# When the gathers of the tile three on are issued in a mixture-of-experts stage: a quarter into the tile instead of at its start

## The chip, the cores and the metric

The kernel runs on one core of a Trainium2 chip. Its engines are named as in the profile: PE (TensorE; PEld is its weight load), DVE (VectorE), ACT (ScalarE), POOL (GpSimd) and SP (SyncE). The metric is the device time of one execution in microseconds; the time before is the median of three runs.

## The reference

A squared-relu attention without softmax makes a gated x, and a mixture of experts with one expert a token is applied to it. Of the reference, cut:

```
scores = (1/S) * z @ z.T                 # B = 8, S = 2496, d_qk = 64
attn   = maximum(scores, 0) ** 2
x      = (u * (attn @ v)).reshape(B*S, 256)

logits = x @ w_gate                      # 8 experts
e      = argmax(logits); gate = softmax(logits)[e]
for each expert e:                       # w1[e]: 256 x 1024, w2[e]: 1024 x 256
    h  = maximum(x[mask] @ w1[e], 0)
    out[mask] = gate[mask] * (h @ w2[e])
```

## The kernel before

The span has two parts. Up to about 1400 us the attention is worked off. Its rows of x (256 numbers, the gate and the token's place, 272 words a row) are written to the DRAM tensor `xrows`, and the tokens are sorted by expert into lists of places. From there to the end the **expert tiles** run, 47 of them in a list `order`, 0 to 46. The first six ("A") are drawn from all sequences but the last, the others ("F") from what remains. A tile is 4, 3 or 2 blocks of 128 tokens of one expert. More tiles follow behind a branch on the number that the data needs; they don't run in the profiled execution.

A tile `i` goes through these steps, each a function:

- `load_w` (L701): an expert's weights come in two halves, each an indirect DMA of 128 × 2048 numbers that POOL issues.
- `load_x(i)` (L711): for each block an indirect DMA, issued by POOL, gathers 128 rows of `xrows` into a buffer `rows`, of which there are three. These are the **gathers**.
- `turn_x(i)` (L742): for each block a transposing DMA, issued by SP, from `rows` to `th`, of which there are three too.
- `take_gates(i)` (L747): DVE copies the gates out of `rows` into `gt`, and with that `rows` is used up.
- `split_x(i)` (L755 and L758 on ACT, L756 and L759 on DVE): the turned halves are put together and split into a high and a low part for PE.
- `split_piece` (L731 to L734): ACT and DVE split a piece of the weights in the same manner.
- `up` (PE L776 into `ph`; then ACT's relu L780 and DVE's subtraction L781, which make its high and low part), `down` (PE L799 for the high part, L802 for the low one, into `y`).
- `finish(i)` (ACT L812, DVE L813, and then L815): the result is weighted with the gates, and for each block POOL issues an indirect DMA that writes 128 rows to the output. These are the **scatters**.

A tile of 4 or 3 blocks has 8 groups of hidden columns, a tile of 2 blocks has 4. The loop in `tiles` goes over tiles and groups, `g` being the group and `G` their number in the tile. In each group PE does `up` for the group two on and `down` for this one. At `g == 0` the weights of the next expert and the gathers of tile `i + 3` are issued, at `g == G // 2` tile `i + 2` is turned and its gates taken, at `g == 0` tile `i + 1` is split, and the last group finishes the tile.

The order of the program is not the order on an engine. Each engine works off its own queue in order, and a scheduler fills these queues: it may put an instruction that stands later in the program ahead of others, as its own reckoning of when operands are ready has it. `pinned(work)` (L350) takes that freedom from what it is given: each instruction is issued behind the last instruction of every engine among the 400 that were written just before. Indirect DMAs all go through POOL's one queue: gathers, scatters and weight halves hold each other up there by their order.

Of the kernel before, what the change touches and what calls it, by code (L numbers as in the profile page):

```python
# [47 lines left out]
def fused_kernel(ctx: ExitStack, tc: tile.TileContext, zt, ut, v, wg, wcat, out):  # L48
# [40 lines left out]
    def ring_rows():  # L89
        return sb.tile([P, QC // P, ROW], I32, name="rows", tag="rows", bufs=3)  # L90

    def ring_sd():
        return sb.tile([P, QC // P, ROW], I32, name="sd", tag="sd")
# [256 lines left out]
    def pinned(work):  # L350

        last = {}
        for i in nc.cur_bb.bb.instructions[-400:]:
            last[i.engine] = i
        with ExitStack() as behind:
            for i in last.values():
                behind.enter_context(tc.issue_after(i))
            work()
# [338 lines left out]
    def load_w(w, h):  # L697
        which, t, _ = order[first_of[w]]
        wr = slot(free[0])
        free.append(free.pop(0))  # L700
        nc.gpsimd.indirect_dma_start(out=wr, out_offset=None, in_=wcat,  # L701
                                     in_offset=bass.IndirectOffsetOnAxis(ap=lists[which]["widx"][:, h, t:t + 1], axis=0))
        weights[w, h] = wr

    def load_x(i):
        which, t, k = order[i]
        src = xrows[0:NTOK - S, :] if which == "A" else xrows

        xg = ring_sd() if i == 0 else ring_rows()
        for s in range(k):  # L710
            nc.gpsimd.indirect_dma_start(out=xg[:, s, :], out_offset=None, in_=src,  # L711
                                         in_offset=bass.IndirectOffsetOnAxis(ap=lists[which]["idx"][:, s, t:t + 1], axis=0))
        xgs[i] = xg

    def split_piece(q):

        i, j = divmod(q, NPC)
        wr = weights[i, j // 2]
        jj = j % 2
        if q % 6 < 5:  # L720
            w1, w2 = ring4(), ring4()
        else:

            if not kept:
                kept.append(free.pop(0))
            w12 = slot(kept[0]).bitcast(FR)
            w1, w2 = [w12[:, k * F:(k + 1) * F].rearrange("p (a b d) -> p a b d", a=2, b=2) for k in range(2)]

        r1 = wr[:, 0:F].rearrange("p (i f) -> p i f", i=2)[:, :, jj * FP:(jj + 1) * FP]
        r2 = wr[:, F:].rearrange("p (c d) -> p c d", d=D)[:, 2 * jj:2 * jj + 2, :]  # L730
        nc.scalar.copy(w1[:, 0], r1)  # L731
        nc.vector.tensor_tensor(w1[:, 1], r1, w1[:, 0].bitcast(F32), op=ALU.subtract)
        nc.scalar.copy(w2[:, :, 0, :], r2)
        nc.vector.tensor_tensor(w2[:, :, 1, :], r2, w2[:, :, 0, :].bitcast(F32), op=ALU.subtract)  # L734
        pieces[q] = w1, w2

    def turn_x(i):

        k = blocks[i]
        tp = ring_halves()  # L740
        for s in range(k):
            nc.sync.dma_start_transpose(out=tp[:, :, s * P:(s + 1) * P], in_=xgs[i][:, s, 0:D].bitcast(U16))  # L742
        turned[i] = tp

    def take_gates(i):
        gates[i] = sb.tile([P, BS], F32, name="gt", bufs=4)
        nc.vector.tensor_copy(gates[i][:, 0:blocks[i]], xgs.pop(i)[:, 0:blocks[i], D].bitcast(F32))  # L747

    def split_x(i):

        n = blocks[i] * P
        tp = turned.pop(i)
        xf = sb.tile([P, 2, QC], F32, name="x", tag="x")
        halves = xf[:, :, :n].bitcast(U16).rearrange("p i (n h) -> p i n h", h=2)
        nc.scalar.copy(halves[:, :, :, 1], tp[:, 0:2, :n])  # L755
        nc.vector.tensor_copy(halves[:, :, :, 0], tp[:, 2:4, :n])  # L756
        xh, xl = ring_hi(), ring_lo()
        nc.scalar.copy(xh[:, :, :n], xf[:, :, :n])  # L758
        nc.vector.tensor_tensor(xl[:, :, :n], xf[:, :, :n], xh[:, :, :n].bitcast(F32), op=ALU.subtract)  # L759
        xts[i] = xh, xl  # L760

    def up(gi):
        i, g = groups[gi]
        n = blocks[i] * P
        w1 = pieces[piece_of[gi]][0]
        xh, xl = xts[i]
        ph = ps1.tile([P, QC], F32, name="ph", tag="ps1")
        m = fs_of[i]
        for c in range(m):
            f = g * m + c  # L770
            fs = slice(f % 2 * P, (f % 2 + 1) * P)
            o = ph[:, c * n:(c + 1) * n]
            p = 0
            for dd in range(2):
                for part, xx in ((0, xh), (0, xl), (1, xh)):
                    nc.tensor.matmul(o, lhsT=w1[:, part, dd, fs], rhs=xx[:, dd, :n], start=p == 0, stop=p == 5)  # L776
                    p += 1
        hh, hl = ring2(), ring2()
        m *= n
        nc.scalar.activation(hh[:, :m], ph[:, :m], AF.Relu)  # L780
        nc.vector.scalar_tensor_tensor(hl[:, :m], ph[:, :m], 0.0, hh[:, :m].bitcast(F32),  # L781
                                                     op0=ALU.max, op1=ALU.subtract)
        return hh, hl

    def down(gi, hh, hl):
        i, g = groups[gi]
        k = blocks[i]
        n = k * P
        w2 = pieces[piece_of[gi]][1]
        if g == 0:  # L790
            yts[i] = [ps2.tile([P, 2, QC], F32, name=f"y{s}", tag="ps2") for s in range(-(-k // 2))]
        for h in (hh, hl):
            for c in range(fs_of[i]):
                f = g * fs_of[i] + c
                for s in range(k):
                    y = yts[i][s // 2][:, s % 2, :]
                    cs = slice(c * n + s * P, c * n + (s + 1) * P)
                    if h is hh:
                        nc.tensor.matmul(y, lhsT=h[:, cs], rhs=w2[:, f % 2].rearrange("p i d -> p (i d)"),  # L799
                                         start=f == 0, stop=False)  # L800
                    else:
                        nc.tensor.matmul(y[:, 0:D], lhsT=h[:, cs], rhs=w2[:, f % 2, 0, :], start=False,  # L802
                                         stop=f == NF - 1)

    def finish(i):
        which, t, k = order[i]
        gt = gates.pop(i)
        yo = ring_f().rearrange("p a (b d) -> p (a b) d", d=D)
        for s in range(k):
            y = yts[i][s // 2][:, s % 2, :]  # L810
            gate = gt[:, s:s + 1]
            nc.scalar.mul(yo[:, s, :], y[:, D:2 * D], gate)  # L812
            nc.vector.scalar_tensor_tensor(yo[:, s, :], y[:, 0:D], gate, yo[:, s, :], op0=ALU.mult, op1=ALU.add)  # L813
        for s in range(k):
            d = nc.gpsimd.indirect_dma_start(  # L815
                out=out, out_offset=bass.IndirectOffsetOnAxis(ap=lists[which]["idx"][:, s, t:t + 1], axis=0),
                in_=yo[:, s, :], in_offset=None, bounds_check=NTOK - 1, oob_is_err=False)
            for o in outs:
                tc.declare_no_dep(d.ins, o.ins, reason="rows are distinct")
            outs.append(d)  # L820
# [93 lines left out]
    def tiles(lo, hi, n_pieces):  # L914

        mine = [gi for gi, (i, _) in enumerate(groups) if lo <= i < hi]
        for gi in mine:
            i, g = groups[gi]
            G = NF // fs_of[i]
            if bg:  # L920
                pinned(bg.pop(0))
            if g == 0:

                for w, h in ((wof[i] + 1, 0), (wof[i] + 1, 1), (wof[i] + 2, 0)):
                    if own[i] and w <= wof[hi - 1] and (w, h) not in weights and (w < NA or i > NA):
                        load_w(w, h)
                if i + 3 < hi:
                    load_x(i + 3)
            ahead = min(gi + LU, mine[-1])
            while n_pieces < min(piece_of[ahead] + LP + 1, NPC * (wof[hi - 1] + 1)):  # L930
                split_piece(n_pieces)
                n_pieces += 1
            if i + 2 < hi and g == G // 2:
                turn_x(i + 2)
                take_gates(i + 2)
            if i + 1 < hi and g == (0 if i else G // 2):
                pinned(lambda: split_x(i + 1))
            if gi + LU <= mine[-1]:
                hs[gi + LU] = up(gi + LU)
            down(gi, *hs.pop(gi))  # L940
            if g == G - 1:
                finish(i)

    tiles(0, NM, n_pieces)
    needed = nc.values_load(lists["F"]["ns"], min_val=0, max_val=NS)

# [56 lines left out]
```

## Time and profile before

| | |
|---|---|
| runs | 2322.43, 2313.3, 2318.6 us; median 2318.6 |
| profiled execution | 2324.7 us, of which 2322.9 are the span |
| granted TensorE clock, mean | 0.994 |
| PE busy | 2278.9 us, 98% |
| DVE busy | 1632.0 us, 70% |
| ACT busy | 1465.3 us, 63% |
| POOL busy | 625.7 us, 27% |
| gathers of F tiles (L711) | 136, 138.9 us of POOL's time |
| scatters (L815) | 136 of F tiles and 24 of A tiles, 143.7 and 25.3 us |
| weight halves (L701), from 1400 us on | 66, 69.5 us |

A view by windows gives each engine's busy time in a stretch of the span. The timeline has one row for an instruction or for a few of a kind in a row: start, duration, engine, line, operation, what is written and read, and in brackets how long the engine stood idle before it and what ended that. "issue" there is time in which the engine waited for nothing that the profile shows. A matmul's end is modelled, so that neighbouring ones overlap by some tenths.

### The profile page before, as it was taken

The page shows a single profiled execution, that of the slowest core. Times are in us where ns is not written, and L with a number is a line of the kernel's source. Part 1 is how long each engine was busy: PE and PEld are TensorE (multiplying, and loading weights), DVE is VectorE, ACT ScalarE, POOL GpSimd, SP SyncE. Part 2 cuts the span into 40 slices and gives each one's busy share as a digit, 9 for nine tenths or more (in the row PEclk, how much of TensorE's full clock was granted, in tenths as well). Part 3 has the DMA queues.
Part 4 walks back from the last instruction along what each step waited for, and adds up shares of the span by engine and source line. Part 5 has one row for each costly group of instructions (what it writes and reads, how often), then busy time and mean ns, then how long its engine had stood idle before and what let it go on. Part 6 is the DMA issues. An engine that isn't in the chain of part 4 may idle for free.

```text
span 2322.9 us, 33688 instructions
## 1 busy us (share of the span) xinstructions
PE 2278.9 (98%) x12320; PEld 1925.6 (83%) x12320; DVE 1632.0 (70%) x2909; ACT 1465.3 (63%) x1985; POOL 625.7 (27%) x626
## 2 busy tenths in 40 slices
PE   9999999999999999999999989899999999999998
PEld 7888888888888888888888877688888888888887
DVE  8868868878778778877878766455566656657554
ACT  8768668677677777767776654355465555546454
POOL 1011111112102102102111244543445435345322
PEclk9999999999999999999999999899999999999999
DMA  6556656657567367467375484654566646457620
GB/s 163 104 92 135 97 86 135 93 95 134 85 105 132 80 116 121 79 118 125 79 114 95 121 176 89 189 123 131 154 152 173 176 128 207 134 146 194 151 89 29
DMA packets 454366, 287.31 MB, mean 124 GB/s; under 512 B 389100, under 2 KB 411130, under 8 KB 444976
## 3 DMA queue, kind: packets, MB, share of 16 engines
q1 hardware_dynamic: 422800, 165.98, 40.0%
q0 software_dynamic: 31392, 119.10, 17.6%
q8 instruction: 98, 1.61, 0.4%
q14 instruction: 76, 0.62, 0.1%
HBM read 149.79 MB, written 43.43 MB: 83 GB/s over the span
## 4 chain that ended last, share of the span: by engine, by line
PE 85%; issue 4%; DMA 3%; ACT 3%; DVE 2%; POOL 1%; another core or an unknown queue 1%; SPq 0%; POOLq 0%; ACTq 0%
PE ph L776 16%; PE acc L343 13%; PE acc L346 13%; PE acc L345 13%; PE y L799 11%; PE y L802 6%; PE ps_s L306 4%; PE ps_s L307 4%; DMA vr<-in_v_dram 2%; PE ps_s L278 2%; PE pt L398 1%; POOL out_dram L815 1%; PE ps_s L312 1%; DMA rows<-xrows,laidx 1%
## 5 line engine op out<-in xcount | busy, mean ns | idle before, releaser
L346 PE MATMUL acc<-thi,t 128*128 128x512 f32 (+1 forms) x1600 | 614.3, 386 | 0.0
L343 PE MATMUL acc<-thi,t 128*128 128x512 f32 (+1 forms) x1600 | 608.0, 392 | 1.1 <-issue 0.7
L345 PE MATMUL acc<-tlo,t 128*128 128x512 f32 (+1 forms) x1520 | 586.0, 386 | 0.1
L781 DVE SCALAR_TENSOR_TENSOR t<-ph,t 128x512 fp32r<-128x512 f32 (+1 forms) x328 | 220.3, 675 | 238.1 <-ACT t L780 192.5
L776 PE MATMUL ph<-thi,t 128*128 128x512 f32 (+2 forms) x1248 | 379.3, 361 | 3.8 <-issue 2.1
L780 ACT ACTIVATE t<-ph 128x512 fp32r<-128x512 f32 (+1 forms) x328 | 191.9, 591 | 289.1 <-PE ph L776 210.4
L346 PEld LDWEIGHTS acc<-thi,t 128*128 128x128 f32 x1600 | 300.2, 188 | 55.3 <-DVE t L140 0.6
L343 PEld LDWEIGHTS acc<-thi,t 128*128 128x128 f32 x1600 | 299.5, 188 | 54.4 <-DVE x L366 1.2
L345 PEld LDWEIGHTS acc<-tlo,t 128*128 128x128 f32 x1520 | 285.6, 188 | 50.8 <-DVE tlo L319 0.7
L476 POOL DMA_INDIRECT lst<-toks,posi x160 | 197.0, 1231 | 468.2 <-DVE posi L468 425.8
L799 PE MATMUL y<-t,t 128*128 128x512 f32 x1062 | 306.3, 397 | 13.5 <-DVE t L734 6.4
L776 PEld LDWEIGHTS ph<-thi,t 128*128 128x128 f32 x1248 | 226.1, 189 | 32.9 <-issue 2.9
L799 PEld LDWEIGHTS y<-t,t 128*128 128x128 f32 x1062 | 191.5, 191 | 48.7 <-ACT t L780 7.8
L776 PE MATMUL ph<-tlo,t 128*128 128x512 f32 (+2 forms) x624 | 225.6, 362 | 0.7 <-issue 0.7
L815 POOL DMA_INDIRECT out_dram<-tf,lfidx x136 | 143.7, 1057 | 273.4 <-DVE tf L813 245.5
L802 PEld LDWEIGHTS y<-t,t 128*128 128x128 f32 x1062 | 175.8, 190 | 35.2 <-DVE t L781 5.7
L802 PE MATMUL y<-t,t 128*128 128x256 f32 x1062 | 185.0, 283 | 3.6 <-DVE t L781 3.6
L315 ACT ACTIVATE tf<-ps_s 128x1024 f32<-128x1024 f32 (+1 forms) x145 | 133.8, 923 | 85.3 <-PE ps_s L307 43.3
L307 PE MATMUL ps_s<-t,t 128*128 128x512 f32 (+1 forms) x480 | 178.9, 376 | 0.0
L380 POOL MEMSET rows<- 128x64 int32 x40 | 6.8, 172 | 581.7 <-DMA xrows<-rows 359.6
L317 DVE CAST thi<-tf 128x1024 fp32r<-128x1024 f32 (+1 forms) x145 | 90.9, 627 | 102.3 <-ACT tf L316 94.5
L711 POOL DMA_INDIRECT rows<-xrows,lfidx x136 | 138.9, 1021 | 50.2 <-issue 38.3
(252 smaller groups left out, 4050.2 us busy)
## 6 DMA issues: line engine op xcount, KB each, us to landing
vr<-in_v_dram SPq DMA_DIRECT2D x80, 256.0 KB
xrows<-rows SPq DMA_DIRECT2D x32, 544.0 KB
u<-in_ut_dram SPq DMA_DIRECT2D x32, 512.0 KB
zr<-in_zt_dram SPq DMA_DIRECT2D x38, 256.0 KB
u<-in_ut_dram SPq DMA_DIRECT2D x8, 448.0 KB
xrows<-rows SPq DMA_DIRECT2D x8, 408.0 KB
rows<-th SPq DMA_TRANSPOSE x160
lst<-toks,posi POOLq DMA_INDIRECT x160
```

The costliest lines, as they stand in the source:

```text
L307: nc.tensor.matmul(ps[:, i, m:n], lhsT=hl_k, rhs=lh_q[:, m:n], start=False, stop=True)
L343: nc.tensor.matmul(acc[d][:, :n], lhsT=vh, rhs=hi[:, i, :n], start=first and i == 0, stop=False)
L345: nc.tensor.matmul(acc[d][:, :n], lhsT=vh, rhs=lo[:, i, :n], start=False, stop=False)
L346: nc.tensor.matmul(acc[d][:, :n], lhsT=vl, rhs=hi[:, i, :n], start=False, stop=last and i == 1)
L476: i = nc.gpsimd.indirect_dma_start(out=lst1, out_offset=bass.IndirectOffsetOnAxis(ap=posi[:m, j:j + 1], axis=0), in_=toks[:m, col + j:col ...
L711: nc.gpsimd.indirect_dma_start(out=xg[:, s, :], out_offset=None, in_=src, in_offset=bass.IndirectOffsetOnAxis(ap=lists[which]["idx"][:, s, ...
L776: nc.tensor.matmul(o, lhsT=w1[:, part, dd, fs], rhs=xx[:, dd, :n], start=p == 0, stop=p == 5)
L780: nc.scalar.activation(hh[:, :m], ph[:, :m], AF.Relu)
L781: nc.vector.scalar_tensor_tensor(hl[:, :m], ph[:, :m], 0.0, hh[:, :m].bitcast(F32), op0=ALU.max, op1=ALU.subtract)
L799: nc.tensor.matmul(y, lhsT=h[:, cs], rhs=w2[:, f % 2].rearrange("p i d -> p (i d)"), start=f == 0, stop=False)
L802: nc.tensor.matmul(y[:, 0:D], lhsT=h[:, cs], rhs=w2[:, f % 2, 0, :], start=False, stop=f == NF - 1)
L815: d = nc.gpsimd.indirect_dma_start(out=out, out_offset=bass.IndirectOffsetOnAxis(ap=lists[which]["idx"][:, s, t:t + 1], axis=0), in_=yo[:, ...
```

## The change

The call `load_x(i + 3)` is taken out of the part for `g == 0`. It now stands behind it under `g == G // 4`, which is the third group of a tile with 8 groups and the second of a tile with 4, and it is wrapped in `pinned`.

```diff
                 for w, h in ((wof[i] + 1, 0), (wof[i] + 1, 1), (wof[i] + 2, 0)):
                     if own[i] and w <= wof[hi - 1] and (w, h) not in weights and (w < NA or i > NA):
                         load_w(w, h)
-                if i + 3 < hi:
-                    load_x(i + 3)
+            if g == G // 4 and i + 3 < hi:
+                pinned(lambda: load_x(i + 3))
             ahead = min(gi + LU, mine[-1])
```

On PE and ACT the order of instructions stays as it was, but for buffer numbers. On POOL it moves. The first place is where the gathers of tiles 6 to 11 stand. In the rows, `rows<-xrows,lfidx` is a gather, `out_dram<-tf` a scatter and `s_` a weight half; the number behind x counts instructions in a row. POOL before, from the gathers of tiles 6 to 9 (6 of them, a weight half, 8 more) over the scatters of tile 3, the gathers of tile 10, the scatters of tile 4 and the gathers of tile 11:

```order
L711 DMA rows<-xrows,lfidx 128x272 x6
L701 DMA s_15482<-in_wcat_dram,lfwidx 128x2048
L711 DMA rows<-xrows,lfidx 128x272 x8
L815 DMA out_dram<-tf,laidx 19968x256 x2
L701 DMA s_15620<-in_wcat_dram,lfwidx 128x2048
L815 DMA out_dram<-tf,laidx 19968x256 x2
L711 DMA rows<-xrows,lfidx 128x272 x2
L815 DMA out_dram<-tf,laidx 19968x256 x4
L711 DMA rows<-xrows,lfidx 128x272 x4
L701 DMA s_15622<-in_wcat_dram,lfwidx 128x2048
```

POOL now, at the same place, from the gathers of tiles 6 and 7 over the scatters of tiles 3 and 4 to the gathers of tiles 8, 9 and 10:

```order
L711 DMA rows<-xrows,lfidx 128x272 x4
L701 DMA s_15482<-in_wcat_dram,lfwidx 128x2048
L711 DMA rows<-xrows,lfidx 128x272 x2
L815 DMA out_dram<-tf,laidx 19968x256 x2
L701 DMA s_15620<-in_wcat_dram,lfwidx 128x2048
L815 DMA out_dram<-tf,laidx 19968x256 x6
L711 DMA rows<-xrows,lfidx 128x272 x8
L701 DMA s_15622<-in_wcat_dram,lfwidx 128x2048
L711 DMA rows<-xrows,lfidx 128x272 x2
L815 DMA out_dram<-tf,laidx 19968x256 x2
```

Six gathers stand ahead of the scatters of tile 3 where fourteen did, and those of tiles 8, 9 and 10 come together behind the scatters of tile 4. The pattern comes back over the list: tiles 12 to 14, 16 to 18, 22 to 24, 26 to 28, 32 to 34, 36 to 38 and 42 to 44 stand together in the same way. The second place is POOL at tiles 12 to 15, before (gathers of tile 12, of 13, of 14, of 15, with scatters of tiles 6, 7 and 8 between them):

```order
L711 DMA rows<-xrows,lfidx 128x272 x4
L701 DMA s_16271<-in_wcat_dram,lfwidx 128x2048
L815 DMA out_dram<-tf,lfidx 19968x256 x2
L711 DMA rows<-xrows,lfidx 128x272 x4
L701 DMA s_16273<-in_wcat_dram,lfwidx 128x2048
L815 DMA out_dram<-tf,lfidx 19968x256 x2
L701 DMA s_16411<-in_wcat_dram,lfwidx 128x2048
L815 DMA out_dram<-tf,lfidx 19968x256 x2
L711 DMA rows<-xrows,lfidx 128x272 x3
L815 DMA out_dram<-tf,lfidx 19968x256 x4
L711 DMA rows<-xrows,lfidx 128x272 x2
L701 DMA s_16413<-in_wcat_dram,lfwidx 128x2048
```

and now, behind the gathers of tile 11 and down to those of tile 14:

```order
L701 DMA s_16271<-in_wcat_dram,lfwidx 128x2048
L815 DMA out_dram<-tf,lfidx 19968x256 x2
L701 DMA s_16273<-in_wcat_dram,lfwidx 128x2048
L815 DMA out_dram<-tf,lfidx 19968x256 x2
L701 DMA s_16411<-in_wcat_dram,lfwidx 128x2048
L815 DMA out_dram<-tf,lfidx 19968x256 x6
L711 DMA rows<-xrows,lfidx 128x272 x8
L701 DMA s_16413<-in_wcat_dram,lfwidx 128x2048
L711 DMA rows<-xrows,lfidx 128x272 x3
L815 DMA out_dram<-tf,lfidx 19968x256 x2
```

Tiles 12 and 13 have moved behind the scatters of tiles 6, 7 and 8, and only a weight half stands between them and tile 14. The third place is DVE at the gates of tile 8. DVE before, from the split of tile 6 on (L756):

```order
L756 COPY x<-th 128x2x256
L747 COPY gt<-rows 128x4
L781 SCALAR_TENSOR_TENSOR t_15303<-ph,t_15302 128x512
L734 TENSOR_TENSOR t_15398<-s_15049,t_15398 128x2x256
L759 TENSOR_TENSOR tlo<-x,thi 128x2x256
L781 SCALAR_TENSOR_TENSOR t_15322<-ph,t_15321 128x512
L732 TENSOR_TENSOR t_15428<-s_15049,t_15428 128x512
```

and now:

```order
L756 COPY x<-th 128x2x256
L781 SCALAR_TENSOR_TENSOR t_15298<-ph,t_15297 128x512
L734 TENSOR_TENSOR t_15398<-s_15049,t_15398 128x2x256
L759 TENSOR_TENSOR tlo<-x,thi 128x2x256
L781 SCALAR_TENSOR_TENSOR t_15322<-ph,t_15321 128x512
L732 TENSOR_TENSOR t_15428<-s_15049,t_15428 128x512
L781 SCALAR_TENSOR_TENSOR t_15341<-ph,t_15340 128x512
L734 TENSOR_TENSOR t_15429<-s_15049,t_15429 128x2x256
L747 COPY gt<-rows 128x4
L732 TENSOR_TENSOR t_15484<-s_15051,t_15484 128x512
L781 SCALAR_TENSOR_TENSOR t_15367<-ph,t_15366 128x512
```

The copy of the gates (L747) has gone back behind two more groups of tile 5. The same copy moves back for tiles 12, 16, 22, 26, 32, 36, 42 and 46; the rest of DVE's order stays, and on SP the transposes of one tile change places with writes of the attention part.

## The prediction

> **What bounds the kernel now.** I read the page's busy times first, then the same times stage by stage.
>
> ```profile
> span 2322.9 us, 33688 instructions
> PE 2278.9 (98%) x12320; PEld 1925.6 (83%) x12320; DVE 1632.0 (70%) x2909; ACT 1465.3 (63%) x1985; POOL 625.7 (27%) x626
> ...
> 1420.00:1500.00 80.00, 69.61 (x339) 56.66 (x337) 50.17 (x175) 32.77 (x56) 40.93 (x40) 0.96 0.53 152
> 1500.00:1600.00 100.00, 95.31 (x482) 80.78 (x483) 50.75 (x85) 45.58 (x81) 39.16 (x37) 0.95 0.53 129
> 1600.00:1700.00 100.00, 97.44 (x507) 82.90 (x506) 55.30 (x93) 50.30 (x90) 41.51 (x40) 0.98 0.49 129
> 2000.00:2100.00 100.00, 99.83 (x557) 87.89 (x557) 60.09 (x103) 54.97 (x99) 45.44 (x45) 1.00 0.53 150
> ```
>
> In the window rows the columns are the stretch, its length, then the busy time (and count) of PE, PEld, DVE, ACT and POOL, the granted clock, the DMA share and GB/s. PE is busy for 98% of the span, so the kernel can gain only where PE stands still or runs at half clock. The expert tiles begin near 1400 us; from 1700 us on PE is nearly full, and what it lacks lies between 1480 and 1660. In ten-microsecond windows:
>
> ```profile
> 1480.00:1490.00 10.00, 8.57 (x41) 6.69 (x39) 4.36 (x7) 1.68 (x3) 7.56 (x9) 1.00 0.97 237
> 1490.00:1500.00 10.00, 2.90 (x8) 2.25 (x8) 2.09 (x5) 1.72 (x4) 6.74 (x7) 0.65 0.81 210
> 1500.00:1510.00 10.00, 7.94 (x31) 6.75 (x32) 2.60 (x5) 2.17 (x4) 1.96 (x2) 0.66 0.24 81
> 1510.00:1520.00 10.00, 10.00 (x51) 8.43 (x50) 2.13 (x4) 2.04 (x4) 0.00 (x0) 1.00 0.00 1
> 1560.00:1570.00 10.00, 7.38 (x27) 5.61 (x28) 4.22 (x8) 3.98 (x9) 4.98 (x6) 0.83 0.97 207
> 1570.00:1580.00 10.00, 10.00 (x53) 8.54 (x52) 7.70 (x11) 6.70 (x11) 2.81 (x3) 1.00 0.86 247
> 1640.00:1650.00 10.00, 7.44 (x28) 5.46 (x27) 4.82 (x9) 3.60 (x8) 5.51 (x6) 0.83 0.70 231
> ```
>
> There are three dips. The full windows behind them hold 51 and 53 matmuls, so one costs 10/51 = 0.196 or 10/53 = 0.189 us, and matmuls missing from a window are time lost, the half clock included. Dip a: (51−41) + (51−8) + (51−31) = 73 missing, 73 × 0.196 = 14.3 us. Dip b: 53−27 = 26, 4.9 us. Dip c: 53−28 = 25, 4.7 us. Together **23.9 us**. What stands in dip a? The timeline of PE and ACT, with a normal pair last:
>
> ```profile
> 1488.18 0.40 PE L776 MATMUL ph<-thi,t 128*128 128x512 f32 x1
> 1494.95 1.19 PE L799 MATMUL y<-t,t 128*128 128x512 f32 x2 [6.38 <-DVE t L734]
> 1502.06 2.07 PE L799 MATMUL y<-t,t 128*128 128x512 f32 x4 [4.21 <-ACT t L780]
> 1501.41 1.57 ACT L780 ACTIVATE t<-ph 128x512 fp32r<-128x512 f32 x3 [6.99 <-remote]
> 1511.01 0.40 PE L776 MATMUL ph<-thi,s 128*128 128x512 f32 x1
> 1511.50 0.60 ACT L780 ACTIVATE t<-ph 128x512 fp32r<-128x512 f32 x1 [2.17 <-PE ph L776]
> ```
>
> In the normal pair ACT starts its relu (L780) 0.1 us after PE's last up-matmul (1511.01 + 0.40 = 1511.41, then 1511.50). In dip a the last up-matmul ends at 1488.58, ACT stands, and its relus run at 1501.41, 12.8 us later; PE has nothing to multiply and its granted clock falls to 0.65. ACT's releaser is called "remote": nothing ACT or DVE did was late. The news from PE reached ACT late. What ran at that time is the longest sequence of gathers in the kernel. Counted by the gathers' line alone (busy POOL time and, in brackets, the number issued):
>
> ```profile
> 1403.00:1414.00 11.00, 7.66 (x8) 1.00 0.83 125
> 1471.00:1492.00 21.00, 14.24 (x14) 1.00 0.73 180
> 1553.00:1573.00 20.00, 8.16 (x8) 0.91 1.04 188
> 1635.00:1651.00 16.00, 5.99 (x6) 0.89 1.00 220
> 1771.00:1785.00 14.00, 7.17 (x7) 1.00 1.02 255
> 2138.00:2156.00 18.00, 8.58 (x8) 1.00 0.75 158
> ```
>
> The run of 14 (tiles 6 to 9) lies against dip a, those of 8 and 6 at 1553 and 1635 on dips b and c. Three other groups of 7 or 8 lost nothing:
>
> ```profile
> 1403.00:1414.00 11.00, 11.00 (x61) 9.36 (x60) 4.62 (x13) 2.99 (x7) 7.66 (x8) 1.00 0.83 125
> 1771.00:1785.00 14.00, 14.00 (x73) 11.85 (x72) 4.59 (x9) 3.75 (x7) 10.18 (x10) 1.00 1.02 255
> 2138.00:2156.00 18.00, 18.00 (x93) 15.26 (x92) 8.82 (x14) 7.83 (x14) 13.31 (x13) 1.00 0.75 158
> ```
>
> So long runs of gathers go with late relus, and short ones sometimes. That is a reading from coincidence: the trace shows no channel by which a gather delays PE's message.
>
> **The change part by part.** It adds and removes no instruction; it moves gathers on POOL. Their own cost is not the matter: POOL is busy 27% and an issue takes about 1 us. By the printed order three things follow.
>
> *Removed, the run of 14.* The gathers of tiles 8 and 9 leave it, six (tiles 6 and 7) remain. The groups at dips b and c go too, as groups of that shape.
>
> *Added, eight longer runs.* The new order lets the gathers of two tiles go after the scatters of one, with the next tile's close behind (one weight half between): tiles 8–10, 12–14, 16–18, 22–24, 26–28, 32–34, 36–38 and 42–44, of 10, 11, 10, 11, 10, 11, 10 and 12 gathers, 85 in all. The trace has no run of 10 to 12. Its price is bounded by the rows above: nothing, as in the groups at 1403, 1771 and 2138, up to the line from groups of 8 to the run of 14. The five groups of 6 to 8 lost 0, 4.9, 4.7, 0 and 0 us: 9.6 us over 37 gathers, 1.9 us a group or 0.26 a gather. From 1.9 at 8 to 14.3 at 14 the line rises by 2.07 a gather, and at 85/8 = 10.6 gathers stands at 7.3 us. I take the lower middle, since 10.6 is nearer to 8 than to 14, in two readings: by the group, (8 new + the six left) × 1.9 = 17.3 us; by the gather, (85 + 6) × 0.26 = 23.7 us. Against the 23.9 us of the dips, which go in full, this gives −6.6 and −0.2 us. I choose halfway: **−3.4 us**.
>
> *Moved, the landing towards its first reader.* The gates of a tile (L747, DVE) read the gathered rows. For nine tiles (8, 12, 16, 22, 26, 32, 36, 42, 46) L747 stands some rows later on DVE, and the gathers just ahead of it. Of a landing, the stall and what it cost the trace has one case, and for tile 8 it has the slots:
>
> ```profile
> 1474.83 1.52 POOL L711 DMA_INDIRECT rows<-xrows,lfidx  x1 [0.30 <-issue]
> 1478.97 0.17 DVE L747 COPY gt<-rows 128x2 f32<-128x2 f32 x1 [3.26 <-DMA rows<-xrows,lfidx]
> 1470.00:1480.00 10.00, 10.00 (x51) 8.25 (x51) 6.74 (x15) 7.37 (x12) 6.55 (x6) 1.00 0.42 108
> 1532.16 1.44 POOL L711 DMA_INDIRECT rows<-xrows,lfidx  x1 [0.30 <-issue]
> 1532.10 0.68 DVE L734 TENSOR_TENSOR t<-s,t 128x512 fp32r<-128x512 f32 x1
> 1534.98 0.69 DVE L781 SCALAR_TENSOR_TENSOR t<-ph,t 128x512 fp32r<-128x512 f32 x1
> ```
>
> Tile 6's second gather was issued at 1474.83 and L747 released at 1478.97: 4.1 us from issue to landing. In the new order tile 8's four gathers take the place of tile 11's behind tile 4's scatters; the fourth is then issued at 1532.16 and lands near 1536.3. L747's slot, behind the L734 at 1532.10, opens at 1532.78: DVE stands about 3.5 us. Behind it wait L732 and then the subtraction L781 of 1534.98, for which PE's L802 waits. I price this at nothing, because the stall of 3.26 us at 1478.97 left PE's window full (10.00). If that cover is gone, it is 9 × 3.5 = 31.5 us. The bound below is nothing too, since DVE gains no time from a later landing.
>
> The transposes (L742, SP) and then the split (L755) read the rows as well. They don't set the end:
>
> ```profile
> 1571.86 1.38 ACT L755 COPY x<-th 128x1024 uint16<-128x1024 uint16 x1
> L742 SPq DMA_TRANSPOSE th<-rows x156: 269/1222/2699, 1379.0 to 2220.9; - x156
> POOL out_dram L815 <- DVE tf L813: 275.6, 49, 17.5
> ```
>
> Four transposes at 1.22 us after 1536.3 are issued by 1541.2, 30 us ahead of tile 8's split at 1571.86: nothing, from either side, unless a transpose took several times the longest of that row (2.7 us). The scatters that are moved ahead of gathers gain nothing either: what they wait for is DVE's L813 (275.6 us in 49 waits), and nothing waits for an output row but the end. The first two tiles of the move (4 and 5, behind tile 0's scatters) fall on the group at 1403, which cost nothing and stays eight long.
>
> The sum is −23.9 + (17.3 to 23.7) + 0, in the middle −3.4. The profiled execution took 2324.7 us (span 2322.9 and 1.8 around it), 6.1 over the median of the runs, 2318.6. From its 2324.7 the sum gives 2321.3; carried over to the median it gives **2315 us**.
>
> **Rivals.** *Free runs (faster).* The new runs cost nothing, as at 1403, 1771 and 2138, where eight gathers and up to two weight halves went by under a full PE; only the 14 was too many. Then 23.9 us come back: 2318.6 − 23.9 = 2295. For it stand three groups of five, and PE's full windows from 1700 on, where the gathers go on. Against it stand dips b and c with 8 and 6 gathers.
>
> *Long runs (slower).* A run of 10 to 12 behaves like that of 14 in its measure, 7.3 us each: 8 × 7.3 + 1.9 − 23.9 = +36.4, or 2355. For it speaks dip a; against it, that the run of dip a began the moment the tile lists were done, so that everything held back by them fell on it, which the later runs don't meet:
>
> ```profile
> 1471.93 1.32 POOL L711 DMA_INDIRECT rows<-xrows,lfidx  x1 [3.95 <-DVE lfidx L655]
> ```
>
> It decides from (11.6 + 23.9 − 1.9)/8 = 4.2 us a run on.
>
> *Late landing (slower).* L747 stands 3.5 us for each of the nine tiles and the subtraction behind it reaches PE late every time: 2315 + 31.5 = 2347. It decides from the point where PE's lead over L781 is shorter than the stall. Against it speaks the absorbed stall of 3.26 us. For it, that in dip b PE stood 2.52 us for a relu, so that delays of a few us do use up its lead:
>
> ```profile
> 1559.99 0.49 PE L776 MATMUL ph<-thi,t 128*128 128x512 f32 x1
> 1563.00 0.72 PE L799 MATMUL y<-s,t 128*128 128x512 f32 x2 [2.52 <-ACT t L780]
> ```
>
> The Trainium skill speaks for this rival: its page "DMA: Bandwidth & Descriptors", section "Rules for kernel authors", says to issue a DMA early, compute, and wait on its semaphore late, so that the fixed cost overlaps. The change issues later with the reader where it was or slightly behind. By that rule the sum would lean to 2347, by the row at 1478.97 to no cost; the trace so far agrees with the row.
>
> *No link (no change).* The dips have nothing to do with gathers, but with the end of the tile lists and the heavy transposes around 1480 to 1650, which the change leaves alone: 2318.6. Against it speak three dips that all lie on groups of gathers.
>
> **How the numbers follow.** Forecast 0.40, free runs 0.25, long runs 0.17, late landing 0.10, no link 0.08. The shown runs span 2313.3 to 2322.4 us, 0.4%, so about 0.5% (11.6 us) is what a measurement can tell from no change: faster is under 2307.0, slower over 2330.2. The forecast alone spans 2303 to 2330 (runs from half of the 17.3 to one and a half times the 23.7, less the dips); of its 0.40 I give 0.04 to faster and 0.03 to slower. Free runs give 0.23 faster and 0.02 the same; long runs 0.16 slower, late landing 0.09 slower, 0.01 each the same; no link 0.08 the same. Together faster 0.27, same 0.45, slower 0.28. The range goes from the free runs to the late landing, 2294 to 2347; outside it lie most of the long runs and the tails of those two, about 0.2.
>
> **What would show it.** Right, if PE's count in the windows of the old dips is back above 50, the gathers on POOL stand in eight runs of 10 to 12, and PE's waits for L780 lie beside some of them and sum to some 20 us with the half clock. Free runs show as full PE windows there; long runs as relus over 5 us late in most of the eight and a clock under 0.9 at each; late landing as DVE's waits of L747 for the gathered rows, a few us each, with PE's L802 waiting for L781. I am wrong from the start if dips stay at 1490 to 1510 with only six gathers there, or if new ones open where no gather runs.

## The result and the profile after

The changed kernel takes 2343.16 us (median of 6 runs, 2337.9 to 2348.98), the kernel before beside it 2319.51 us (6 runs). The ratio is **1.0112, 95% interval 1.0094 to 1.0129: slower by 24 us**. The forecast of 2315 us was wrong, its range (to 2347) held the time. The page of the profiled execution, the lowest of the six:

```profile
span 2336.2 us, 33615 instructions
...
PE 2287.4 (98%) x12320; PEld 1932.7 (83%) x12320; DVE 1631.5 (70%) x2909; ACT 1465.5 (63%) x1985; POOL 628.9 (27%) x626
```

The windows of the changed kernel, first where dips a and b were, then four in which PE now falls behind (columns as in the prediction):

```profile
1480.00:1490.00 10.00, 10.00 (x52) 8.46 (x51) 6.43 (x11) 5.53 (x11) 3.55 (x4) 1.00 0.87 202
1490.00:1500.00 10.00, 10.00 (x53) 8.53 (x52) 3.99 (x8) 2.60 (x5) 5.01 (x5) 1.00 0.60 185
1560.00:1570.00 10.00, 10.00 (x53) 8.50 (x52) 7.33 (x11) 6.34 (x11) 1.22 (x1) 1.00 0.59 169
...
1430.00:1440.00 10.00, 6.67 (x33) 5.38 (x33) 1.71 (x9) 2.92 (x5) 5.65 (x6) 0.98 0.91 117
1440.00:1450.00 10.00, 9.07 (x38) 7.10 (x38) 9.79 (x54) 3.70 (x8) 3.64 (x4) 0.85 0.58 132
1690.00:1700.00 10.00, 5.09 (x17) 3.49 (x16) 2.48 (x4) 2.95 (x6) 3.78 (x4) 0.78 1.04 169
2080.00:2090.00 10.00, 8.03 (x29) 6.55 (x30) 5.04 (x9) 4.78 (x10) 0.73 (x1) 0.66 0.86 148
```

The old dips are full windows of 52 and 53 matmuls. Of the new ones, those at 1690 and 2080 lie on two of the eight runs; those at 1430 and 1440 lie on the gathers of tiles 4 and 5, which come up again below. Counted by the gathers' line alone, four of the eight:

```profile
1600.00:1625.00 25.00, 10.49 (x11) 0.93 0.83 167
1680.00:1705.00 25.00, 9.80 (x10) 0.86 0.82 156
2065.00:2090.00 25.00, 9.85 (x10) 0.86 0.74 160
2180.00:2205.00 25.00, 12.55 (x12) 0.93 0.79 157
```

At 1690, PE stands between its own matmuls for nothing that the profile shows, and ACT waits 9 us for a semaphore that PE's matmuls raise (timeline of PE, then of ACT):

```profile
1692.71 0.28 PE L802 MATMUL y<-t,t 128*128 128x256 f32 x1 [1.49 <-issue]
1694.36 0.33 PE L776 MATMUL ph<-thi,t 128*128 128x384 f32 x1 [1.38 <-issue]
1696.03 0.48 PE L776 MATMUL ph<-tlo,t 128*128 128x384 f32 x1 [1.33 <-issue]
...
1696.73 0.62 ACT L731 CAST t<-s 128x512 fp32r<-128x512 f32 x1 [9.03 <-remote]
```

And the gathers now land late for their readers. DVE's and SP's waits, from 1400 us on (in total, times, longest):

```profile
DVE gt L747 <- DMA rows<-xrows,lfidx: 20.8, 9, 4.1
...
DVE gt L747 <- DMA rows<-xrows,laidx: 8.3, 1, 8.3
...
SPq L742 <- DMA rows<-xrows,lfidx: 508.7, 30, 45.5
```

Before, SP's transposes waited above all for a buffer that DVE's split set free, as SP's waits of the kernel before show:

```profile
SPq L742 <- DVE x L756: 277.2, 24, 28.4
```

Now they wait for gathers, so that a tile's transposes run while the next tile's gathers are in flight.

To price single dips I compared traces matmul by matmul: all of these programs have the same 12320 matmuls in the same order on PE, and the start of the n-th in one trace less that in another says how much was lost up to there. The reference is the kernel before in a later comparison, in which it has no dip at all (told below). In us:

```
                      up to 1395   1395 to 1450   behind 1450   all
before                    2.3           6.3            29.5     38.1
changed                   5.0           7.7            39.1     51.8
```

Dips a, b and c come out at 14.6, 5.0 and 4.7. The eight runs cost 3.9, 4.5, 8.4, 3.6, 1.7, 1.9, 8.0 and 4.5 us: 36.5 together, **4.6 each**. The two profiled executions are 13.7 us apart by this, the medians 24: the profiled execution of the changed kernel is the lowest of its six runs, and that of the kernel before (2324.7 us) lies above all six of its own.

### The profile page after: what moved, and what is told of

It is laid out like the page before. It is cut to its first block, busy times and chain, and to the rows that moved or that the text cites. A ratio compares the mean times of both kernels' runs of the same rounds, so it can differ in the third digit from the quotient of the medians.

```text
span 2336.2 us, 33615 instructions
## 1 busy us (share of the span) xinstructions
PE 2287.4 (98%) x12320; PEld 1932.7 (83%) x12320; DVE 1631.5 (70%) x2909; ACT 1465.5 (63%) x1985; POOL 628.9 (27%) x626
## 4 chain that ended last, share of the span: by engine, by line
PE 86%; DMA 4%; issue 3%; DVE 3%; ACT 2%; POOL 1%; another core or an unknown queue 0%; SPq 0%; POOLq 0%; ACTq 0%; DVEq 0%
PE ph L776 17%; PE acc L343 13%; PE acc L346 13%; PE acc L345 13%; PE y L799 12%; PE y L802 6%; PE ps_s L306 4%; PE ps_s L307 4%; DMA vr<-in_v_dram 2%; PE ps_s L278 2%; PE pt L398 1%; DMA rows<-xrows,laidx 1%; PE ps_s L312 1%; DMA s<-th 0%; DVE tlo L280 0%
## 5 line engine op out<-in xcount | busy, mean ns | idle before, releaser
L776 PE MATMUL ph<-thi,t 128*128 128x512 f32 (+2 forms) x1248 | 384.9, 365 | 10.1 <-issue 5.7
```

## The experiments

**Which part of the edit does it.** The edit has two parts, the later call and the pin.

```diff
+            if g == G // 4 and i + 3 < hi:
+                load_x(i + 3)                       # e1: later, not pinned
```

> The gathers are issued a quarter into the tile, but not pinned. By the printed order POOL's and SP's queues are then row for row those of the kernel before, so the scheduler puts an unpinned gather back to where it was. Theory 'order' (the time follows the order on POOL's queue, not the place in the program): 2319 us as before, dips at 1490, 1560 and 1640. Rival 'place' (the later call itself costs the time, for instance through DVE's and SP's order): near the changed kernel's 2343.

```diff
                 if i + 3 < hi:
+                    pinned(lambda: load_x(i + 3))   # e2: pinned, not later
```

> The gathers stay at the tile's beginning, but are pinned. By the printed order POOL's and SP's queues are row for row those of the changed kernel. Theory 'order': 2343 us as the changed kernel, with the eight runs of 10 to 12 gathers and a dip at most of them. Rival 'place': 2319.

Without the pin: 2312.8 us beside 2313.4, ratio 0.999 (0.9969 to 1.0012). With the pin at the old place: 2335.7 us, 1.0092 (1.0062 to 1.0122), behind 1450 a loss of 37.1 us. In the traces every engine's work stands in the order of the kernel before without the pin, and in that of the changed kernel with the pin at the old place. So the quarter of a tile in the change's name does nothing. The scheduler moves a free gather back to where it was; the pin alone puts it behind the scatters, and these wait for DVE.

Both are thus the two orders once more. The eight runs again cost 4.6 us each. The old order differs more from its first profile: without the pin, dip a costs 10.5 us in place of 14.6, dips b and c 2.3 and 1.3, and 8.3 us are lost from 1410 to 1430, behind the group at 1403 that the prediction counted as free. Two windows of that kernel:

```profile
1420.00:1430.00 10.00, 6.91 (x18) 4.80 (x18) 6.20 (x20) 5.31 (x8) 2.25 (x3) 0.68 0.29 46
...
1490.00:1500.00 10.00, 3.27 (x11) 2.75 (x11) 4.21 (x9) 3.55 (x8) 5.07 (x6) 0.77 0.67 161
```

So the price of one group changes from execution to execution.

**What in the runs costs time.** From here on the changed kernel is altered. One transpose a tile:

```diff
-        for s in range(k):
+        for s in range(k if i < 6 else 1):          # in turn_x; the split reads block 0 for all
             nc.sync.dma_start_transpose(...)
```

> The changed kernel with one transposing DMA a tile in place of two to four from tile 6 on (every block then reads block 0's turned rows, so x is wrong for the others; the same instructions on ACT, DVE and PE). Gathers, scatters and weight halves stand as in the changed kernel. Theory 'meeting' (PE's messages come late where the transposes of one tile run while the gathers of the next are in flight, which the changed order brings about at each of the eight runs): the dips go, 2295 to 2305 us. Rival 'long runs' (10 to 12 gathers in a row do it alone): the dips stay, 2335 to 2345. Rival 'late landing' (DVE standing at the gates' copy holds PE up): they stay too, and DVE's waits for the gathered rows stay near 20 us.

One gather a tile, and half of them:

```diff
-        for s in range(k):
+        for s in range(k if i < 6 else 1):          # e4; e6: else (k + 1) // 2
             nc.gpsimd.indirect_dma_start(...)       # in load_x; the transposes read what is there
```

> The changed kernel with one gather a tile in place of two to four from tile 6 on (transposes and gates of all blocks read block 0's rows, so x is wrong for the others); all transposes, scatters and weight halves stay. Theories 'meeting' and 'long runs': the dips go, 2295 to 2305 us. Rival 'transposes alone' (eight to ten transposes back to back do it without gathers): the dips stay at 2330 or more, and DVE hardly waits for gathered rows.

> The changed kernel with half the gathers of a tile from tile 6 on (2 of 4, 2 of 3, 1 of 2; the other blocks read the gathered ones, so x is wrong for them). The eight runs are then of 5 or 6 gathers. 'Long runs' with a price by the gather: half of the 40 us that the runs cost are left, near 2315. 'Long runs' with a threshold, as three of five groups of 6 to 8 in the kernel before suggest: 2295 to 2302.

With one transpose a tile it is 1.0064 (1.0046 to 1.0081), and 31.3 us are lost behind 1450, beside 37.1 for the pin alone: the dips don't need the transposes, which at most make them somewhat dearer (the intervals of the two ratios overlap), and "meeting" falls as the main cause. With one gather a tile it is 0.9913 (0.9883 to 0.9942), and PE stands nowhere behind 1450, though every transpose, scatter and weight half is there. Two windows of that kernel:

```profile
1600.00:1700.00 100.00, 100.00 (x553) 87.67 (x551) 63.55 (x108) 57.91 (x103) 32.54 (x32) 1.00 0.56 150
...
2000.00:2100.00 100.00, 100.00 (x553) 87.91 (x552) 62.81 (x107) 56.90 (x101) 34.50 (x32) 1.00 0.59 155
```

With half of the gathers it is 0.9931 (0.9907 to 0.9954), with 1.4 us lost behind 1450. Runs of 5 or 6 are as good as free, so the price isn't a fixed one for each gather.

Next the length, in two ways. Only tile 8's gathers pinned in the kernel before, which sets a run of 14 at another place:

```diff
+                if i + 3 in (8,):
+                    pinned(lambda: load_x(i + 3))
+                elif i + 3 < hi:
                     load_x(i + 3)
```

> The kernel before with the gathers of tile 8 alone pinned. By the printed order POOL then has 6 gathers where 14 stood, and a run of 14 (10, a weight half, 4: tiles 8 to 11) behind the scatters of tile 4; from tile 12 on it is the order before. If the loss is by the run's length, dip a moves to about 1530 and keeps its size: 2313 as before. If dip a was due to what was held back by the lists, the new run costs what the changed kernel's do, about 5 us: 2303.

The ratio is 1.000 (0.9984 to 1.0016). Dip a is gone from 1490, and the new run of 14 has a dip of its own. That kernel's gathers and windows at that place:

```profile
1505.00:1530.00 25.00, 14.00 (x14) 0.86 0.77 178
```

```profile
1505.00:1530.00 25.00, 16.43 (x84) 13.54 (x82) 6.36 (x11) 4.77 (x9) 17.49 (x18) 0.86 0.77 178
```

It costs 11.7 us; dip a was not owed to the lists. The other way leaves out each expert's second weight half:

```diff
+        if w >= 5 and h == 1:                       # in load_w of the changed kernel
+            weights[w, h] = weights[w, 0]
+            return
```

> The changed kernel without the second weight half of each expert from the sixth on (the first half is used twice, so the result is wrong). The eight runs stay, 10 or 11 gathers without a break, with one weight half and 2 to 4 gathers behind; half of the weight traffic is gone. If a run needs the weight halves beside it to slow PE, the dips go: 0.991 to 0.995 of before. If gathers alone do it, each unbroken run costs at least what it did: 1.008 to 1.013.

Here less traffic made it much slower: 2381.5 us, 1.0292 (1.026 to 1.0324). POOL's queue no longer stops for a weight half inside the runs; eight of them hold 10 to 12 gathers without a break and 13 to 15 in all. The gathers and the windows of one, and ACT in it:

```profile
1690.00:1715.00 25.00, 11.89 (x13) 0.80 0.86 172
```

```profile
1690.00:1715.00 25.00, 14.71 (x65) 12.21 (x64) 6.05 (x11) 5.53 (x10) 12.84 (x14) 0.80 0.86 172
```

```profile
1709.14 0.62 ACT L734 CAST t<-s 128x512 fp32r<-128x512 f32 x1 [13.32 <-remote]
```

Its runs cost 9.9, 8.4, 13.2, 8.5, 9.2, 6.6, 13.7 and 9.3 us. With these the price by length can be set side by side, in us a run. A run is counted across a weight half between its gathers; the second row's groups have scatters between them too, and are priced by the prediction's windows:

```
gathers in the run   in which kernel                  runs   loss a run
5 or 6               half the gathers                   8      0.2
6 to 8               before (the prediction's five)     5      1.9
10 to 12             changed; pin alone                 8      4.6; 4.6
10 to 12             changed order, in e5 (below)       8      6.6
13 to 15             one weight half an expert          8      9.9
14                   only tile 8 pinned                 1     11.7
14                   before, dip a; the same in e1      1     14.6; 10.5
```

On average the price rises with the length: next to nothing at 5 or 6 gathers, 4.6 to 6.6 us at 10 to 12, some 10 to 15 at 13 to 15. The length doesn't set it alone. Single runs of ten in the changed kernel cost 1.7 to 8.4 us, its run of twelve 4.5, and every price here is that of one profiled execution.

**Late landing.** Twice the copy of the gates was to be moved back, first by its place in the program only, then pinned behind the split:

```diff
-                take_gates(i + 2)
+            if i + 2 < hi and g == G - 1:           # e5
+                take_gates(i + 2)
```

> The changed kernel with the copy of the gates moved from the middle group of a tile to its last one; the transposes and POOL's order stay. Theory 'long runs' (each run of 10 to 12 gathers makes PE's steps and messages slow, 4 to 5 us a run by the changed kernel's matmuls against those of the kernel with one gather a tile): no change, 2333 to 2343 us. Rival 'late landing': DVE's 21 us of waits for the gathered rows go, and with them 10 us or more of the time: 2325 or less.

```diff
                 pinned(lambda: split_x(i + 1))
+                pinned(lambda: take_gates(i + 1))   # e9
```

> The changed kernel with the copy of a tile's gates pinned behind the split of its rows, so that it stands on DVE behind instructions that need the same gathers (and their transposes) anyway; moving it to the tile's last group without a pin had left DVE's 20 us of waits for gathered rows in place. If late landing is part of the cost, as the evenly spaced gathers suggest (three dips there begin with 5 to 7 us of DVE standing at this copy), the waits at the copy go and 5 to 15 us of the changed kernel's 22 to 24 with them: ratio to before 1.003 to 1.008. If the cost is the runs of gathers alone: ratio 1.009 to 1.012.

The first left DVE's waits at 20.5 us and took 1.0134 (1.0108 to 1.016). In its trace every engine's work stands in the order of the changed kernel: the scheduler had put the copy back, as it had the free gather. So it says nothing on late landing; it is the changed order a third time, 32 us over before, and its profiled execution loses 58.3 us behind 1450 where the others of that order lose 39.1 and 37.1. The second took the waits away and 1.006 (1.0034 to 1.0086): 14 us over before in place of 22 to 32. Its profiled execution loses 36.8 us behind 1450, so that a gain from the F tiles' waits doesn't show in its matmuls. With that spread for one order, and with an interval that overlaps that of the pin alone (1.0062 to 1.0122), what the late landing costs beside the runs stays open here.

**Spacing.** Each gather at its own group, made to wait for DVE's newest subtraction; then the same with the gates behind the split:

```diff
+            if i + 3 < hi:
+                some = [s for s in range(blocks[i + 3]) if s * G // blocks[i + 3] == g]
+                if some:
+                    load_x(i + 3, some, ups[-1])    # waits for the newest L781
```

> The kernel before with each gather of tile i + 3 issued at its own group of tile i, spread evenly, and made to wait for DVE's subtraction of the newest group, so that POOL can't send a tile's gathers in one go. 'Long runs': no run of 10, the dips go, 2296 to 2303 us, faster than both kernels. Rival 'late landing' or 'any gather': as many gathers land later than before, 2313 or more.

> The kernel with evenly spaced gathers, its copy of the gates moved in the same manner. If its dips were late landings at that copy, they go, and with neither long runs nor late landings the time is that of the kernel with one gather a tile: 0.990 to 0.994 of before, faster than both kernels. If any dense stretch of gathers and weight halves slows PE, it stays within 0.3% of before.

Spaced alone: 0.9997 (0.9984 to 1.001), no gain. Its largest dips are another thing. The gates' copy (line 753 there) and PE at one of them:

```profile
1749.64 0.17 DVE L753 COPY gt<-rows 128x2 f32<-128x2 f32 x1 [6.89 <-DMA rows<-xrows,lfidx]
```

```profile
1750.45 0.51 PE L808 MATMUL y<-t,t 128*128 128x256 f32 x2 [3.28 <-DVE t L787]
```

A stall of 6.9 us at the copy does reach PE. With the copy behind the split it is 2304.4 us beside 2314.2, **0.9964 (0.9948 to 0.998), a little faster than the kernel before**, and so than the changed one; 13.7 us are still lost behind 1450, where before lost 29.5.

**A comparison without dips.** To tell the issuing of gathers from the rows that they bring, all gathers of the changed order were issued, but most with 32 rows:

```diff
+            n = P if i < 6 or s == 0 else 32
+            nc.gpsimd.indirect_dma_start(out=xg[:n, s, :], ...)
```

> The changed kernel's POOL order with all its gathers issued, but from tile 6 on only the first gather of a tile brings 128 rows and the others bring 32 each, which nobody reads (transposes and gates of all blocks read block 0, so x is wrong for the others): runs of 10 to 12 issues with somewhat less than half of the rows. If it is the issuing of gathers one after the other that slows PE, the runs cost what they do in the changed kernel: ratio to before 1.005 to 1.012. If it is the rows that they bring, it is like the kernel with half the gathers or one gather a tile: 0.990 to 0.995.

It had no dip behind 1450 (0.0 us lost), but took 2298.4 us beside 2284.9 of the kernel before, which had taken 2313 to 2320 in every comparison so far. So both kernels, the short gathers and the spaced ones went side by side:

> The kernel before once more, for its profile on the chip of this comparison. On the last chip it took 2285 us where five others gave 2313 to 2320. If the dips are the whole of that difference, a chip with 2285 shows windows without dips a, b and c, and a chip with 2313 to 2320 shows them again.

> The changed kernel once more on the same chip. If the interference of gathers with PE depends on the chip: on a chip with 2285 before, no dip at the eight runs, and only what late landing costs (ratio 1.003 to 1.006); on a chip with 2313 to 2320, the eight dips and 1.009 to 1.013. If it does not depend on the chip: the eight dips on either.

> The runs of 10 to 12 issues with less than half of the rows, beside the changed kernel on the same chip. If issuing is what slows PE: within 5 us of the changed kernel. If the rows are: 15 us or more below it, provided that the changed kernel has its dips on this chip; without them nothing is told apart.

> The evenly spaced gathers with the copy of the gates behind the split, on the same chip. On a chip where the kernel before has its dips, 0.993 to 0.998 of it; on one where it has none, 1.000 to 1.003.

The kernel before took 2285.1 us again and the changed one 2292.6, **1.0032 (1.0022 to 1.0043)**; the short gathers took 1.0057 (1.004 to 1.0074), of which some 7 us lie behind the last matmul, and the spaced ones 1.0003 (0.9994 to 1.0013). Here the kernel before sends the same run of 14 gathers:

```profile
1462.00:1484.00 22.00, 14.37 (x14) 1.00 0.85 182
```

```profile
1462.00:1484.00 22.00, 22.00 (x114) 18.51 (x113) 13.49 (x25) 11.68 (x20) 17.13 (x17) 1.00 0.85 182
```

PE is full. The changed kernel's first run of ten, and what remains of its loss:

```profile
1512.00:1530.00 18.00, 9.62 (x10) 1.00 0.79 175
```

```profile
1425.00:1435.00 10.00, 5.50 (x25) 4.46 (x24) 2.46 (x12) 2.01 (x5) 3.69 (x4) 0.88 0.90 130
...
1512.00:1530.00 18.00, 18.00 (x115) 16.29 (x115) 11.80 (x20) 11.96 (x22) 12.38 (x13) 1.00 0.79 175
```

Behind 1450 the changed kernel loses 0.0 us in this comparison. So the price of a run hangs on something that differs between comparisons, and the short gathers tell nothing apart there: issuing or rows stays open.

That it is the chip, as the expectations had it, is not shown. The chips of the comparisons with dips are numbered 6, 2 and 13 (that of the first is not given; so three or four chips, not the five of the expectation), those of the comparisons without 1, 2 and 1: number 2 is on both sides, with 2319.6 and 2285.8 us for the kernel before. All comparisons with dips came before all without.

One thing else goes with the difference. A trace holds records of semaphores that landing DMAs raise. The thirteen traces of the comparisons with dips have 13.2 to 14.6 thousand of them each, the seven of the others 18.8 to 18.9 thousand. The number of DMAs isn't the reason: the kernel before has the same in both, and has 3797 of these records from 1400 us on where it has dips, 8302 where it has none. So more than half are missing there, and they are missing too where a kernel of those comparisons has no dip (4584 with one gather a tile). Whether what loses the records also holds up PE's signals, so that the recording itself has a part in the dips, was not tested.

What the changed kernel does lose without dips is one stall, in its own timeline on POOL, DVE and PE:

```profile
1408.32 1.00 POOL L815 DMA_INDIRECT out_dram<-tf,laidx  x1 [13.97 <-DVE tf L813]
...
1419.44 1.09 POOL L711 DMA_INDIRECT rows<-xrows,laidx  x1 [0.30 <-issue]
...
1432.54 0.17 DVE L747 COPY gt<-rows 128x4 f32<-128x4 f32 x1 [9.65 <-DMA rows<-xrows,laidx]
...
1433.36 1.22 PE L802 MATMUL y<-t,t 128*128 128x256 f32 x4 [4.50 <-DVE t L781]
```

Tile 4's gathers now stand behind tile 0's scatters, which wait 14 us for DVE, and behind the lists' scatters. DVE stands 9.7 us at tile 4's gates, and PE 4.5 us for the subtraction queued behind. At the other copies DVE waits 26.1 us in all, never over 4.2, and PE not at all:

```profile
DVE gt L747 <- DMA rows<-xrows,lfidx: 26.1, 10, 4.2
...
DVE gt L747 <- DMA rows<-xrows,laidx: 9.7, 1, 9.7
```

**The two halves.** Last, the pin for the tiles from 6 on alone, and for those before it alone:

```diff
+                if i + 3 < hi and i + 3 >= 6:       # e17; e18: i + 3 < 6
+                    pinned(lambda: load_x(i + 3))
+                elif i + 3 < hi:
                     load_x(i + 3)
```

> The kernel before with the gathers pinned from tile 6 on; those of tiles 3 to 5 stay ahead of tile 0's scatters. From tile 6 on POOL's order is the changed kernel's, so the eight runs are there; the 8 to 10 us that DVE stands at the copy of tile 4's gates are not. On a chip where the kernel before has its dips (2313 to 2320): the changed kernel less 7 us, 1.005 to 1.008 of before. On one without (2285): 0.999 to 1.001.

> The other part alone: the gathers of tiles 3 to 5 pinned, those of tile 6 on as before. Tile 4's gathers stand behind tile 0's scatters, which wait for DVE's L813, and land late. On either chip PE loses 4 to 8 us near 1430 for it: 1.002 to 1.0035 of before; if that stall is made up later, 1.000.

Both fell into a comparison without dips, with 2286 us before. From tile 6 on: 1.000 (0.9992 to 1.0009), with the eight runs and 25.5 us of waits at the gates. Before tile 6: 2291.6 us, 1.0025 (1.0014 to 1.0036), a loss of 5.6 us by the matmuls. PE from 1400 us on in the second, and a window of the first:

```profile
PE y L802 <- DVE t L781: 3.6, 1, 3.6
```

```profile
1425.00:1435.00 10.00, 10.00 (x51) 8.40 (x50) 9.38 (x51) 5.22 (x11) 2.99 (x3) 1.00 0.08 27
```

So without the dips the whole loss of the change is tile 4's late landing. That the eight runs alone cost 1.005 to 1.008 where there are dips was not tried; the pin alone and the table above are what bears on it.

## Why the prediction was wrong, by its steps

*The reading of the dips* held: three dips on groups of gathers, and 23.9 us for them. They went with the run of 14 and the old groups, and where gathers were taken out nothing else made a dip. "No link" fell, in the comparisons that have dips. That three groups were free was the luck of one execution: the same order in another lost 8.3 us behind one of them.

*"Added, eight longer runs"* is **the step that failed**. It saw the eight runs and bounded their price from 0 to 7.3 us, and then took the lower middle, 1.9 a group or 0.26 a gather, because 10.6 is nearer to 8 than to 14. They cost 4.6 us each in two executions and 6.6 in a third, over the 4.2 from which the rival "long runs" was to decide. Together that is 36.5, against the 17.3 to 23.7 of the sum, with the six gathers left. The error was to carry an average over groups of 6 to 8, three of which were free, to a length beyond all of them, when the one longer run in the trace cost four times as much for each gather. The line between the ends gave 7.3 and was too high, but on the right side. The rival's own signs came in part: ACT stood over 5 us in four of the eight runs, and the clock of a run's 25 us went under 0.9 in two. What makes a run of gathers cost time, and only in some comparisons, neither the prediction nor the runs tell.

*"Moved, the landing"* was half right. For the nine F tiles nothing was to be paid, and in the comparison without dips DVE's 26 us of waits there cost PE nothing. But the sentence on tiles 4 and 5, that their group "cost nothing and stays eight long", looked at the length only. Their gathers had come to stand behind scatters that wait for DVE; the first copy that needs them stood 8 to 10 us, and PE lost 6. The rival "late landing" named the right mechanism, put it at nine places where it was free without dips, and not at the one where it wasn't. Its measure, PE's lead over the subtraction, holds without dips: stalls of up to 4.3 us were hidden, those of 9 to 10 were not. With dips one of 6.9 us reached PE too.

*"Moved, the transposes"* held for its own sum: behind 1450 no split waited for them. They had become a neighbour of the gathers, but leaving all but one a tile out took the loss behind 1450 only from 37.1 to 31.3 us, less than one order varies.

By its own terms the sum should have read, where there are dips: −24.3 for the dips and +36.5 for the runs, or +12, and up to 6 more for tile 4, of which the two profiled executions show 1.4 (7.7 against 6.3 between 1395 and 1450). These executions are 13.7 us apart; the medians say 24, and the rest is not explained by these traces.

## What to carry to other kernels

An order on one queue has a length: before moving instructions, count how many of a kind now go out without a break, and price the new length between the short runs and the longest one in the trace, not from the mean of the short ones alone. Look at what a moved instruction comes to stand behind, and whether that waits: here one reader that stood 9.7 us cost PE time, and ten that stood 4.2 or less cost none. And if only a pin moves a call, its place in the program is not what was changed: two edits here that moved a call without one left every engine's order as it was.

## What the runs showed of the hardware

In the same program and, by the windows, with the same gathers in flight, a run of 14 gathers cost PE 10 to 15 us in some comparisons and nothing in others: 2313 to 2320 us for the kernel before in four comparisons, 2285 to 2286 in three. All but 2.3 of the 38.1 us lie behind the point where the gathers of the expert tiles begin to overlap with PE's work. Where it costs, a semaphore that PE raises reaches ACT up to 13 us late and PE itself pauses 1 to 2.5 us between its own matmuls. Which path it is that the gathers fill there, whether issuing them or their rows do it, and what differs between the comparisons (the chip, the time, the recording of the profile) is open. A ratio measured once for such a change need not hold in the next comparison: it was 1.011 here and 1.003 there.
